# Collecting all output terms of a decode kernel in one PSUM bank, and multiplying the last matrix as it lands

## The chip, the cores and the metric

The kernel runs on one core of one Trainium2 chip. The metric is device time in microseconds (us), lower is better. Spans in a profile are a little shorter than the measured time (416.8 us of span beside 418.6 us). Each run of a changed kernel was taken on the same chip beside runs of the kernel before, and all runs quoted are marked fast in the record: none was more than 1.5% above the fastest of its kernel.

## The reference

One token passes through two branches whose results are added. Branch A is attention over a cache: 32 query heads share 4 key/value heads, with 65,536 cached positions of 128 numbers each. Branch B is a small MLP mixer. Everything is bf16.

```python
def _A_ref(x, k_cache, v_cache, wq, wo):           # x: 1 x 1 x 1024
    q = (x @ wq).reshape(1, 1, 32, 128)...
    p = softmax(q k^T * 128 ** -0.5)                 # 4 kv heads x 65536 positions
    return (p v).reshape(1, 1, 4096) @ wo            # wo: 4096 x 1024

def _B_ref(x, w1, w2, w3, w4):
    h = gelu(layernorm(x) @ w1)
    hs = shift(h) @ w2                               # one token: every shift moves in zeros
    x1 = x + hs
    return x1 + gelu(layernorm(x1) @ w3) @ w4        # w4: 3584 x 1024

xn = layernorm(x)
out = x + _A_ref(xn, ...) + _B_ref(xn, ...)
```

The caches are 134 MB, all matrices 36 MB. Each number is used once or a few times, so the transfers set the pace.

## The kernel before

Queues of operations are built per engine. `_deps` puts a wait into an engine's queue for every earlier writer and reader of a buffer. Note what it does not do: it does not leave out the engine's own semaphore. When a group of TensorE matmuls writes a buffer that the group before it, also on TensorE, wrote, TensorE waits for its own counter, that is until the earlier group is complete.

```python
def _deps(q, reads, writes):
    for b in reads:
        for s, v in b.w.items():
            q.wait((s, v))
    for b in writes:
        for s, v in b.w.items():
            q.wait((s, v))
        for s, v in b.r.items():
            q.wait((s, v))


def _done(ev, reads, writes, partial=False):
    for b in reads:
        b.add_read(ev)
    for b in writes:
        if partial:
            b.add_write(ev)
        else:
            b.set_write(ev)


def _op(q, fn, reads=(), writes=(), partial=False):
    _deps(q, reads, writes)
    ev = q.op(fn, True)
    _done(ev, reads, writes, partial)
    return ev


def _grp(q, fns, reads=(), writes=(), partial=False):
    _deps(q, reads, writes)
    ev = None
    for i, fn in enumerate(fns):
        ev = q.op(fn, i == len(fns) - 1)
    _done(ev, reads, writes, partial)
    return ev
```

The cache is handled in 32 blocks, eight for each kv head. After the last block of a head, `combine_1` and `combine_2` turn the running sums into that head's eight output columns `OTh_bf[:, h, :]`. They wait for `O_acc`, which GpSimd (POOL) finishes.

```python
def combine_1(h):
    _op(q_pe, lambda e: e.matmul(M0_ps[:, 0:1], Dmat_f[:, :], O_acc[:, 512:513], start=True, stop=True),
        reads=[b_Oacc, b_const], writes=[b_M0])
    _op(q_dve, lambda e: e.reciprocal(cb_rL[:, :], M0_ps[:, 0:1]), reads=[b_M0], writes=[b_cb])
    _op(q_dve, lambda e: e.tensor_scalar(out=cb_W4[:, :, :], in0=maskT[:, :, :], scalar1=cb_rL[:, 0:1], scalar2=None, op0=ALU.mult),
        reads=[b_cb, b_const], writes=[b_cb])

def combine_2(h):
    fns = []
    for t in range(4):
        fns.append(lambda e, t=t: e.matmul(M0_ps[:, 8:8 + G], O_acc[:, t * P:(t + 1) * P], cb_W4[:, t, :], start=(t == 0), stop=(t == 3)))
    _grp(q_pe, fns, reads=[b_Oacc, b_cb], writes=[b_M0])
    _op(q_dve, lambda e, h=h: e.tensor_copy(OTh_bf[:, h, :], M0_ps[:, 8:8 + G]), reads=[b_M0], writes=[b_OTh[h]])
```

The output projection takes one "wo row" at a time (128 x 1024 of `wo`): eight matmuls with the weights as stationary operand and one column as moving operand, all into one PSUM bank, one group for each row. I call these one-column matmuls.

```python
def wo_pe(h, g, src=None):
    if src is None:
        ws_ = (h * G + g) % NWO
        view, bufs = wo_sb[:, ws_, :], [b_wo[ws_]]
    else:
        view, bufs = src
    fns = []
    for ncx in range(KT_D):
        fns.append(lambda e, ncx=ncx, g=g, h=h, view=view: e.matmul(OA_ps[:, ncx:ncx + 1], view[:, ncx * P:(ncx + 1) * P], OTh_bf[:, h, g:g + 1],
                                                                  start=(g == 0 and ncx == 0), stop=(g == G - 1), skip_group_check=True))
    _grp(q_pe, fns, reads=bufs + [b_OTh[h]], writes=[b_OA], partial=(g > 0))
    if g == G - 1:
        _op(q_dve, lambda e: e.tensor_tensor(out=acc[:], in0=acc[:], in1=OA_ps[:, 0:KT_D], op=ALU.add), reads=[b_OA, b_acc], writes=[b_acc])
```

The w4 product has the same form. It comes in seven chunks of 512 x 1024, each one group of 32 matmuls.

```python
def mm_interleaved(ps_tile, col0, ncols, chunks, rhs_fn, b_rhs, b_ps, kt0=0, nkt_total=None):
    nkt = nkt_total if nkt_total is not None else sum(c[2] for c in chunks)
    first = (kt0 == 0)
    kt = kt0
    for sl, lhs_fn, kts in chunks:
        fns = []
        for kk in range(kts):
            for ncx in range(ncols):
                fns.append(lambda e, kk=kk, ncx=ncx, kt=kt, st=(first and kk == 0 and ncx == 0), lhs_fn=lhs_fn:
                           e.matmul(ps_tile[:, col0 + ncx:col0 + ncx + 1], lhs_fn(kk, ncx), rhs_fn(kt + kk),
                                    start=st, stop=(kt + kk == nkt - 1), skip_group_check=True))
        _grp(q_pe, fns, reads=sl.bufs + [b_rhs], writes=[b_ps], partial=not first)
        first = False
        kt += kts
```

At the end of the program, after the last head's combination, stand ten wo rows, then the seven w4 chunks, then an add, a transpose, a copy and the store:

```python
for (h_, g_) in wo_tail:
    wo_pe(h_, g_, src=wo_tail_src[(h_, g_)])
mm_interleaved(H2_ps, 0, KT_D, chunks_of("w4"), lambda kt: gh_bf[:, kt:kt + 1], b_gh, b_H2)
_op(q_dve, lambda e: e.tensor_tensor(out=fin[:], in0=acc[:], in1=H2_ps[:, 0:KT_D], op=ALU.add), reads=[b_acc, b_H2], writes=[b_fin])
_op(q_pe, lambda e: e.transpose(out=M0_ps[0:KT_D, 300:300 + P], in_=fin[:, :], identity=ident_f[:, :]), reads=[b_fin, b_const], writes=[b_M0])
_op(q_dve, lambda e: e.tensor_copy(orow[:, :], M0_ps[0:KT_D, 300:300 + P]), reads=[b_M0], writes=[b_orow])
```

```python
# ... cuts
ev_out = _dma(q_sp, ch_out, lambda e: e.dma_start(out=out[0, 0, :].rearrange("(kt p) -> kt p", p=P), in_=orow[:, :]), reads=[b_orow])
```

## Time and profile before

| | before |
|---|---|
| median of the first three runs | 418.62 us (418.47 to 418.73) |
| span of the profiled run | 416.8 us |
| moved from HBM | 169.9 MB, 408 GB/s over the span |
| last w4 chunk landed | about 406.7 us (issue at 385.2, landing 21.5 later) |
| last output matmul ended | about 414.2 us |

The slices of the page cut the span into 40 equal parts. A digit of 9 in the DMA row means that the transfer engines were at least 90% busy. PEclk is the clock granted to TensorE, in tenths.

```profile
span 416.8 us, 5862 instructions
...
PEclk9999955565565565555655555555555566556555
DMA  7999999999999999999999999999999999999980
GB/s 282 426 420 418 425 424 431 424 425 433 428 425 426 425 426 422 422 417 422 426 431 424 426 424 425 416 426 425 426 425 423 425 424 423 427 417 414 424 366 2
```

The transfers are full from the second slice to the 38th. Only the last two slices, about 21 us, are anything else: in the 39th the rate falls, in the 40th nearly nothing moves. What can be gained without moving fewer bytes lies there.

The timeline of the tail gives start (us), duration (us), engine, line, operation, output and inputs, and the idle time before with its releaser. PE stands for TensorE's matmuls, PEld for its weight loads, DVE for VectorE, POOL for GpSimd and SPq for the queue that issues transfers; "issue" means that the profile shows nothing that was waited for.

```profile
396.58 0.37 PE L558 MATMUL OA_ps<-OTh_bf,wo_sb 128*128 128x1 bf16 x8
...
398.52 0.59 PE L537 MATMUL M_ps<-O_acc,Dmat_f 128*128 128x1 f32 x2 [1.56 <-POOL O_acc L533]
...
399.64 1.88 PE L546 MATMUL M_ps<-cb_W,O_acc 128*128 128x8 f32 x8 [0.54 <-DVE cb_W L540]
...
402.58 0.35 PE L558 MATMUL OA_ps<-OTh_bf,WS 128*128 128x1 bf16 x8 [0.35 <-DVE acc L562]
...
406.08 0.35 PE L558 MATMUL OA_ps<-OTh_bf,WS 128*128 128x1 bf16 x8
...
406.29 0.99 PE L388 MATMUL H_ps<-gh_bf,WS 128*128 128x1 bf16 x32
...
413.13 0.99 PE L388 MATMUL H_ps<-gh_bf,Vn 128*128 128x1 bf16 x32
414.23 0.16 DVE L724 TENSOR_TENSOR fin<-acc,H_ps 128x8 f32<-128x8 f32 x1 [7.60 <-PE H_ps L388]
...
414.86 0.28 DVE L726 CAST orow<-M_ps 8x128 bf16<-8x128 f32 x1 [0.47 <-PE M_ps L725]
415.17 0.31 SPq L739 DMA_DIRECT2D out_dram<-orow  x1
```

The wo rows of the last head start after the combination, one every 0.50 us (0.35 of matmuls, the rest a gap). The first w4 chunk is multiplied at 406.29 us although it landed near 392.0. From there seven chunks take 1.14 us each, to 414.2 us.

The view of waits, for the weight loads of TensorE (PEld; total us, times, longest), shows the gaps of the wo rows without naming a cause:

```profile
PEld OA_ps L558 <- issue: 2.9, 10, 0.8
```

A stretch of the tail (us from and to, length, then busy us and number of instructions for PE, PEld, DVE, ACT and POOL, then the granted clock, DMA share and GB/s) shows the transfers running out while TensorE goes on at a clock of 0.50:

```profile
404.00:408.00 4.00, 3.17 (x94) 2.92 (x95) 0.16 (x1) 0.00 (x0) 0.00 (x0) 0.50 0.28 117
```

### The profile page before, as it was taken

To read this page: it belongs to the slowest core of one execution; us is meant where nothing else is said; L and a number is where in the kernel's file an instruction comes from. 1 tells how busy PE (TensorE), PEld (TensorE's weight loads), DVE (VectorE), ACT (ScalarE), POOL (GpSimd) and SP (SyncE) were. 2 spreads that over 40 slices of the span, in tenths; PEclk is the share of its full clock that TensorE was granted. 3 is DMA by queue.
4 is the path that set the end of the run, shared out by engine and by line. 5 is a ranking of instruction groups with operands and counts; after the bars stand their busy time and mean duration, and the time that the engine had idled before them with its cause. 6 is when DMAs were issued, how large, how long until landed. Compare 5 with 4: busy or idle time off the path is not lost.

```text
span 416.8 us, 5862 instructions
## 1 busy us (share of the span) xinstructions
PE 192.5 (46%) x2333; PEld 92.2 (22%) x2333; DVE 202.8 (49%) x369; ACT 84.7 (20%) x159; POOL 60.8 (15%) x86
## 2 busy tenths in 40 slices
PE   1532444434047646424464553345457543333566
PEld 1420111111015312101123221112224111111256
DVE  2037665625466476543345555344556655554200
ACT  0000322312122042221222221122222222121300
POOL 4000011111011121111110111111110111111210
PEclk9999955565565565555655555555555566556555
DMA  7999999999999999999999999999999999999980
GB/s 282 426 420 418 425 424 431 424 425 433 428 425 426 425 426 422 422 417 422 426 431 424 426 424 425 416 426 425 426 425 423 425 424 423 427 417 414 424 366 2
DMA packets 30330, 170.24 MB, mean 408 GB/s; under 512 B 2272, under 2 KB 2272, under 8 KB 23776
## 3 DMA queue, kind: packets, MB, share of 16 engines
q1 hardware_dynamic: 30304, 169.88, 97.8%
q8 instruction: 18, 0.29, 0.3%
q14 instruction: 8, 0.07, 0.0%
HBM read 169.87 MB, written 0.00 MB: 408 GB/s over the span
## 4 chain that ended last, share of the span: by engine, by line
DMA 43%; SPq 36%; PE 7%; DVE 6%; issue 4%; ACT 2%; POOL 0%; POOLq 0%; ACTq 0%; DVEq 0%
DMA Kn<-in_A_k_cache_dram 43%; SPq L435 22%; SPq L429 6%; SPq L422 4%; DVE X L448 3%; PE OT_ps L519 2%; ACT p_sb L490 2%; PE H_ps L388 2%; DVE mrow L467 1%; SPq L673 1%; SPq L342 1%; PE OA_ps L558 1%; PE M_ps L546 1%; PE PTB_ps L504 1%; SPq L579 1%
## 5 line engine op out<-in xcount | busy, mean ns | idle before, releaser
L448 DVE STREAM_TRANSPOSE X<-Kn 128x1024 f32<-128x1024 f32 x128 | 151.3, 1221 | 131.4 <-DMA Kn<-in_A_k_cache_dram 131.3
L490 ACT ACTIVATE p_sb<-S_ps,brun 128x512 bf16<-128x512 f32 x32 | 44.6, 1395 | 179.2 <-DVE brun L488 156.7
L519 PE MATMUL OT_ps<-Vn,pT_sb 128*32 128x512 bf16 x512 | 60.8, 627 | 22.0 <-ACT pT_sb L509 22.0
L460 PE MATMUL S_ps<-X,Yall 128*32 128x512 bf16 x512 | 59.1, 607 | 6.9 <-DVE X L448 6.9
L473 PE MATMUL PTB_ps<-Rm,Lmat 128*128 128x16 bf16 x32 | 6.2, 194 | 107.1 <-DVE Rm L468 107.1
L504 PE MATMUL PTB_ps<-ident_bf,p_sb 128*128 128x128 bf16 x128 | 19.2, 305 | 58.0 <-ACT ff L498 54.8
L533 POOL TENSOR_TENSOR O_acc<-O_acc,tmpO 128x513 f32<-128x513 f32 x28 | 32.8, 1172 | 88.5 <-ACT tmpO L527 88.5
L531 POOL TENSOR_SCALAR O_acc<-O_acc,ff 128x513 f32<-128x513 f32 x28 | 19.5, 698 | 169.1 <-ACT ff L498 169.1
L473 PEld LDWEIGHTS PTB_ps<-Rm,Lmat 128*128 128x128 bf16 x32 | 3.3, 104 | 131.7 <-DVE Rm L468 131.7
L527 ACT ACTIVATE tmpO<-OT_ps 128x512 f32<-128x512 f32 x32 | 19.1, 598 | 64.0 <-PE OT_ps L519 64.0
L519 PEld LDWEIGHTS OT_ps<-Vn,pT_sb 128*32 128x32 bf16 x512 | 14.9, 128 | 47.3 <-ACT pT_sb L509 30.4
L504 PEld LDWEIGHTS PTB_ps<-ident_bf,p_sb 128*128 128x128 bf16 x128 | 10.9, 129 | 60.6 <-ACT ff L498 57.3
L467 DVE TENSOR_REDUCE mrow<-S_ps 128x1 f32<-128x512 f32 x32 | 21.0, 657 | 5.7 <-PE S_ps L460 5.5
L509 ACT ACTIVATE pT_sb<-PTB_ps 128x512 bf16<-128x512 bf16 x32 | 19.1, 597 | 22.3 <-PE PTB_ps L504 22.3
L460 PEld LDWEIGHTS S_ps<-X,Yall 128*32 128x32 bf16 x512 | 15.9, 130 | 28.8 <-issue 21.5
L558 PEld LDWEIGHTS OA_ps<-OTh_bf,wo_sb 128*128 128x128 bf16 x176 | 6.4, 105 | 18.4 <-issue 18.4
L490 ACT ACT_TABLE_LOAD x1 | 1.3, 1283 | 43.3 <-DVE brun L485 43.3
L477 DVE TENSOR_REDUCE Bst<-PTB_ps 128x1 f32<-128x16 f32 x32 | 5.6, 175 | 8.4 <-PE PTB_ps L473 8.4
L529 POOL COPY O_acc<-tmpO 128x513 f32<-128x513 f32 x4 | 2.5, 614 | 48.4 <-ACT tmpO L527 48.4
L388 PE MATMUL H_ps<-xn_bf,WS 128*128 128x1 bf16 x224 | 8.6, 172 | 0.0
L490 ACT ACTIVATION_READ_ACCUMULATOR p_sb<-S_ps,brun 128x1 f32 x32 | 8.3, 259 | 0.0
L558 PE MATMUL OA_ps<-OTh_bf,wo_sb 128*128 128x1 bf16 x176 | 8.2, 168 | 0.0
(107 smaller groups left out, 123.2 us busy)
## 6 DMA issues: line engine op xcount, KB each, us to landing
Kn<-in_A_k_cache_dram SPq DMA_DIRECT2D x32, 2048.0 KB, 23.1
Vn<-in_A_v_cache_dram SPq DMA_DIRECT2D x32, 2048.0 KB, 26.3
WS<-in_B_w_dram SPq DMA_DIRECT2D x8, 896.0 KB, 19.2
wo_sb<-in_A_wo_dram SPq DMA_DIRECT2D x22, 256.0 KB, 25.2
WS<-in_B_w_dram SPq DMA_DIRECT2D x5, 1024.0 KB, 23.5
WS<-in_A_wq_dram SPq DMA_DIRECT2D x4, 1024.0 KB, 8.2
X<-in_A_wq_dram SPq DMA_DIRECT2D x4, 1024.0 KB, 17.0
Kn<-in_B_w_dram SPq DMA_DIRECT2D x4, 1024.0 KB, 15.9
```

What stands on the lines that cost most here:

```text
L429: _dma(q_sp, ch_v[s], lambda e, s=s, n=n: e.dma_start(out=Vn[:, s, :, :, :].rearrange("p a t d -> p a (t d)"), in_=kv_src(A_v_cache, n).re ...
L435: _dma(q_sp, ch_wo[ws_], lambda e, h=h, g=g, ws_=ws_: e.dma_start(out=wo_sb[:, ws_, :], in_=A_wo[(h * G + g) * DH:(h * G + g + 1) * DH, :] ...
L448: _op(q_dve, lambda e, ix=ix, ks=ks, xs=xs: e.transpose(out=X32[:, xs, 1024 * ix:1024 * (ix + 1)], in_=Kn32[:, ks, 16 * ix:16 * (ix + 1), ...
L460: fns.append(lambda e, we=we, c_mid=c_mid, mv=mv, h=h: e.matmul(S_ps[32 * c_mid:32 * c_mid + 32, :], Yall[:, h, we, :, :].rearrange("p a g ...
L467: _op(q_dve, lambda e, m=m: e.reduce_max(mrow[:, m:m + 1], S_ps[:, :], axis=AX.X), reads=[b_S], writes=[b_mrow[m]])
L490: _op(q_act, lambda e, n=n, m=m, kn=kn: e.activation(p_sb[:, m, :].rearrange("p (cl p0 ch) -> p cl ch p0", cl=4, p0=32), S_ps[:, :].rearra ...
L504: fns.append(lambda e, c2=c2, m=m: e.transpose(out=PT_ps[:, c2 * P:(c2 + 1) * P], in_=p_sb[:, m, c2 * P:(c2 + 1) * P], identity=ident_bf[:]))
L509: _op(q_act, lambda e, m=m: e.activation(pT_sb[:, m, :, :, :].rearrange("p r c g -> p c r g"), PT_ps[:, 0:512].rearrange("p (c r g) -> p c ...
L519: fns.append(lambda e, r=r, q4=q4, m=m, vs=vs: e.matmul(OT_ps[32 * q4:32 * q4 + 32, :], pT_sb[:, m, r, :, :].rearrange("p c g -> p (c g)") ...
L527: _op(q_act, lambda e, m=m: e.activation(tmpO[:, m, 0:512], OT_ps[:, :], ACTF.Copy), reads=[b_OT], writes=[b_tmpO[m]], partial=True)
L531: _op(q_pool, lambda e, m=m: e.tensor_scalar(out=O_acc[:, :], in0=O_acc[:, :], scalar1=ff[:, m, 0:1], scalar2=0.0, op0=ALU.mult, op1=ALU.add),
L533: _op(q_pool, lambda e, m=m: e.tensor_tensor(out=O_acc[:, :], in0=O_acc[:, :], in1=tmpO[:, m, :], op=ALU.add), reads=[b_tmpO[m]], writes=[ ...
```

## The change

The intent is to shorten that tail in three ways. All output terms (wo rows, w4 rows, residual) accumulate in one PSUM bank as rows, so that no separate add and transpose is needed: the activation column becomes the stationary operand, and the weights stream past it in four column strips of the array, 256 columns each, into partitions 0, 32, 64 and 96. W4 chunks 0 to 3 are multiplied before the last head's combination is complete. The output is copied from the bank and stored from its four rows.

```diff
@@ -345,6 +343,30 @@
             reads=[b_x8, b_const], writes=[b_M0])
         _op(q_dve, lambda e: e.tensor_copy(xT[:], M0_ps[:, 160:160 + KT_D]), reads=[b_M0], writes=[b_xT])
 
+        _op(q_dve, lambda e: e.memset(OUT_ps[:, :], 0.0), writes=[b_OUT])
+        out_started = [False]
+
+        def out_rows(items, reads, last=False):
+            fns = []
+            for lhs, view in items:
+                for jj in range(4):
+                    st = not out_started[0]
+                    fns.append(lambda e, lhs=lhs, view=view, jj=jj, st=st, last=last: e.matmul(
+                        OUT_ps[32 * jj:32 * jj + 1, 0:256], lhs, view[:, 256 * jj:256 * jj + 256],
+                        start=st, stop=last, tile_position=(0, 32 * jj), skip_group_check=True))
+                out_started[0] = True
+            _grp(q_pe, fns, reads=reads, writes=[b_OUT], partial=True)
+
+        def out_resid():
+            fns = []
+            for kt in range(KT_D):
+                jj, half = divmod(kt, 2)
+                fns.append(lambda e, kt=kt, jj=jj, half=half: e.matmul(
+                    OUT_ps[32 * jj:32 * jj + 1, half * P:(half + 1) * P], acc[:, kt:kt + 1], ident_f[:, :],
+                    start=False, stop=False, tile_position=(0, 32 * jj), skip_group_check=True))
+            assert out_started[0]
+            _grp(q_pe, fns, reads=[b_acc, b_const], writes=[b_OUT], partial=True)
+
         ln_uid = [0]
 
         def layer_norm(src, b_src, dst_f, dst_bf, b_dst, keep=None):
@@ -553,13 +575,7 @@
                 view, bufs = wo_sb[:, ws_, :], [b_wo[ws_]]
             else:
                 view, bufs = src
-            fns = []
-            for ncx in range(KT_D):
-                fns.append(lambda e, ncx=ncx, g=g, h=h, view=view: e.matmul(OA_ps[:, ncx:ncx + 1], view[:, ncx * P:(ncx + 1) * P], OTh_bf[:, h, g:g + 1],
-                                                                          start=(g == 0 and ncx == 0), stop=(g == G - 1), skip_group_check=True))
-            _grp(q_pe, fns, reads=bufs + [b_OTh[h]], writes=[b_OA], partial=(g > 0))
-            if g == G - 1:
-                _op(q_dve, lambda e: e.tensor_tensor(out=acc[:], in0=acc[:], in1=OA_ps[:, 0:KT_D], op=ALU.add), reads=[b_OA, b_acc], writes=[b_acc])
+            out_rows([(OTh_bf[:, h, g:g + 1], view)], bufs + [b_OTh[h]])
 
         def mk_loads(name, w, nkt, per):
             ncol = w.shape[1]
@@ -705,7 +721,7 @@
             PV(n)
             FLASH(n)
             run_pending(n, "c")
-            if nb == NB - 1:
+            if nb == NB - 1 and n + 1 < NBLK:
                 at(n + 1, "a", lambda h=h: combine_1(h))
                 at(n + 1, "b", lambda h=h: combine_2(h))
 
@@ -718,25 +734,28 @@
-        for (h_, g_) in wo_tail:
+        w4_ch = chunks_of("w4")
+
+        def w4_pe(i):
+            sl, _, kts = w4_ch[i]
+            kt = sum(c[2] for c in w4_ch[:i])
+            out_rows([(gh_bf[:, kt + kk:kt + kk + 1], sl.view[:, kk * D:(kk + 1) * D]) for kk in range(kts)],
+                     sl.bufs + [b_gh], last=(i == len(w4_ch) - 1))
+
+        for (h_, g_) in wo_tail[0:2]:
             wo_pe(h_, g_, src=wo_tail_src[(h_, g_)])
-        mm_interleaved(H2_ps, 0, KT_D, chunks_of("w4"), lambda kt: gh_bf[:, kt:kt + 1], b_gh, b_H2)
-        _op(q_dve, lambda e: e.tensor_tensor(out=fin[:], in0=acc[:], in1=H2_ps[:, 0:KT_D], op=ALU.add), reads=[b_acc, b_H2], writes=[b_fin])
-        _op(q_pe, lambda e: e.transpose(out=M0_ps[0:KT_D, 300:300 + P], in_=fin[:, :], identity=ident_f[:, :]), reads=[b_fin, b_const], writes=[b_M0])
-        _op(q_dve, lambda e: e.tensor_copy(orow[:, :], M0_ps[0:KT_D, 300:300 + P]), reads=[b_M0], writes=[b_orow])
... (the debugging taps, removed)
-        ev_out = _dma(q_sp, ch_out, lambda e: e.dma_start(out=out[0, 0, :].rearrange("(kt p) -> kt p", p=P), in_=orow[:, :]), reads=[b_orow])
+        out_resid()
+        for i in range(3):
+            w4_pe(i)
+        combine_1(HKV - 1)
+        w4_pe(3)
+        combine_2(HKV - 1)
+        for (h_, g_) in wo_tail[2:]:
+            wo_pe(h_, g_, src=wo_tail_src[(h_, g_)])
+        for i in range(4, len(w4_ch)):
+            w4_pe(i)
+        _op(q_dve, lambda e: e.tensor_copy(orow[:, :], OUT_ps[:, 0:256]), reads=[b_OUT], writes=[b_orow])
+        ev_out = _dma(q_sp, ch_out, lambda e: e.dma_start(out=out[0, 0, :].rearrange("(j n) -> j n", j=4), in_=orow[0:97:32, :]), reads=[b_orow])
```

Declarations (the bank `OUT_ps` in place of `OA_ps` and `H2_ps`, `orow` of 128 x 256) are left out.

More of the change, by code (lines that the diff above doesn't have):

```diff
@@ L234, in bass_parallel_sum__gqa_block_cached__mixer_s_mlp__decode_kernel @@
         gh_bf = sb("gh_bf", [P, KT_F], BF)
-        fin = sb("fin", [P, KT_D], F32)
-        orow = sb("orow", [KT_D, P], BF)
+        orow = sb("orow", [P, 256], BF)
         H3_ps = ps("H3_ps", [P, 512], F32)
-        H2_ps = H3_ps[:, 32:64]
-        OA_ps = ps("OA_ps", [P, 512], F32)
+        OUT_ps = ps("OUT_ps", [P, 512], F32)
         S_ps = ps("S_ps", [P, 512], F32)
@@ L265, in bass_parallel_sum__gqa_block_cached__mixer_s_mlp__decode_kernel @@
         b_X = [[_B() for _ in range(4)] for _ in range(2)]
-        b_H3 = _B(); b_H2 = _B(); b_tmpO = [_B(), _B()]
+        b_H3 = _B(); b_tmpO = [_B(), _B()]
         b_S = _B(); b_PT = _B(); b_MB = _B(); b_OT = _B()
@@ L275, in bass_parallel_sum__gqa_block_cached__mixer_s_mlp__decode_kernel @@
         b_wo = [_B() for _ in range(NWO)]
-        b_OA = _B()
+        b_OUT = _B()
         b_cb = _B()
@@ L608, in chunks_of @@
             return res
-        b_h1 = _B(); b_x1 = _B(); b_xn3 = _B(); b_gh = _B(); b_fin = _B(); b_orow = _B()
+        b_h1 = _B(); b_x1 = _B(); b_xn3 = _B(); b_gh = _B(); b_orow = _B()
         def mlp_early_1():
@@ L726, in bass_parallel_sum__gqa_block_cached__mixer_s_mlp__decode_kernel @@
-        _op(q_dve, lambda e: e.tensor_copy(orow[:, :], M0_ps[0:KT_D, 300:300 + P]), reads=[b_M0], writes=[b_orow])
-        if dbg:
-            taps = dict(xn=xn[:, :], qT_bf=qT_bf[:, :], Bst=Bst[:, :], Lst=Lst[:, :], O_acc=O_acc[:, :], maskT=maskT[:, :, :].rearrange("p t g -> p (t g)"),
-                        OTh_bf=OTh_bf[:, :, :].rearrange("p h g -> p (h g)"), acc=acc[:, :], fin=fin[:, :], p_sb=p_sb[:, :, :].rearrange("p m k -> p (m k)"),
-                        pT_sb=pT_sb[:, :, :, :, :].rearrange("p m r c g -> p (m r c g)"), hsT=x1[:, :], h1g=h1g_bf[:, :], gh=gh_bf[:, :],
-                        Yall=Yall[:, :, :, :, :].rearrange("p h w a g -> p (h w a g)"), X=X[:, 0, :], Lmat=Lmat[:, :], sel16=sel16[:, :], selG=selG_f[:, :])
-            ch_dbg = _DmaChan(sem("d_dbg"))
-            for qq in (q_pe, q_dve, q_act):
-                q_pool.wait((qq.sem, qq.cnt))
-            for name, dap in dbg.items():
-                src = taps[name]
-                _dma(q_pool, ch_dbg, lambda e, dap=dap, src=src: e.dma_start(out=dap, in_=src))
-                q_pool.wait((ch_dbg.sem, 16 * ch_dbg.n))
```

## The prediction

> **What bounds the kernel now.** The transfer queue, until the last twelve microseconds. The slices show DMA at 9 tenths and about 425 GB/s throughout; the stretches view gives DMA share 1.01 up to 402 us, 0.04 after 406. The rest of the 416.8 us span is a tail that TensorE bounds. By issue and landing, the seven w4 chunks land at about 392.0, 394.5, 396.9, 399.3, 401.8, 404.3 and 406.7 us. None is multiplied before 406.3: all stand behind the last head's wo rows, which stand behind that head's combination. The chain of waits: PV ends 396.65, O_acc ready 398.48, combination to 401.5, wo rows to 406.4 (0.36 + 0.14 us of gap each), seven w4 chunks to 414.2 (1.00 + 0.14 us each), add, transpose and copy to 415.14, store to 416.8.
>
> **What the change does.** The activation column becomes the stationary operand and the weights stream as rows: 4 matmuls of 256 columns in four column strips for 8 of one column. W4 chunks 0 to 3 fill the wait for the combination; the add and the transpose go.
>
> Cost of a row: the score matmuls, also in four strips, do 16 x 512 columns in 1.90 us at granted clock 0.50 (timeline), so strips run side by side (the Trainium skill, "TensorEngine Tiling (Array Packing)", Theoretical Speedup, says up to 4x; this agrees). So 4 x 256 columns should cost 1.90/8 = 0.24 us, an estimate: hardly less than the 0.28 us of a w4 row now, half the 0.50 us of a wo row. The gain is mostly order.
>
> New tail at clock 0.5 (estimates from those durations): the loop's wo row and two tail rows to 397.4; residual, 8 fp32 matmuls, about 2 us (least certain), to 399.4; w4 0-2 to 402.2; combine_1 0.6; w4 3 to 403.7; combine_2 1.9 to 405.6; cast 0.2; eight wo rows to 407.8; w4 4-6 to 410.5. Then the copy of 128x256 from PSUM, about 0.4 us (128x128 took 0.29), and the store's 1.66: span about 412.7, 4 us less.
>
> Clock: it rises to 1.0 at 343.6 and 377.7 us, each time after 3.4 us that PV and score matmuls filled over 93%; 77 to 80% did not raise it. The Trainium skill, "TensorE: Matmul & The Clock Gate", Part 1, gives such a window of about 3.4 us; the trace agrees. The old tail stayed at 0.5. The new one streams long rows, so the clock may rise near 401.6 us; if it holds, the matmuls end near 408, soon after the last landing. I give that even odds, in part or in full.
>
> Nothing else should move: transfers and what frees their buffers are unchanged, and the new memset (about 0.5 us) falls in a prologue waiting for wq.
>
> **Predicted: 413.4 us, 8 in 10 between 411.3 and 415.9.** Faster by over 2%: 0.03; within 2%: 0.96; slower by over 2%: 0.01. The last landing plus a last chunk, copy and store leaves about 411, so 2% is almost out of reach.
>
> **Right if** the last transfer still lands near 406.5; four w4 chunks precede combine_2; a w4 chunk takes 0.85-1.0 us (half if the clock rises); from the last matmul to the end is about 2.1 us, was 2.6.
>
> **Wrong if** the fp32 residual takes over 3.5 us; one-column stationary operands stop the strips from overlapping (a row would cost 0.9 us: slower by 15 us); switching between strips and full array drains the array; or the loop's shorter rows change the transfer stream.

## The result, and the profile after

| | before | after |
|---|---|---|
| median (same rounds) | 418.68 us (418.47 to 418.81, 4 runs) | 417.79 us (417.14 to 418.11, 4 runs) |
| ratio | | 0.998, 95% interval 0.9966 to 0.9994 |
| span of the profiled run | 416.8 us | 416.3 us |
| TensorE instructions (matmuls and loads) | 4666 | 4216 |
| last output matmul ended | 414.2 us | 413.7 us |
| from there to the end | 2.6 us | 2.6 us |

Ratios in this document are the mean time of one kernel's fast runs over that of the other's of the same rounds, so they are not quite the ratio of the medians.

The change is faster by 0.2%, where 1.3% was forecast. The slices after show the same stream of transfers:

```profile
span 416.3 us, 5407 instructions
...
PEclk9999996655655565666555555665555555665656
DMA  7999999999999999999999999999999999999990
GB/s 276 427 422 424 425 425 433 421 424 436 425 428 422 425 424 421 424 418 424 425 433 420 427 424 419 424 424 426 426 422 425 425 425 422 426 420 413 425 379 3
```

The tail after (columns as above):

```profile
396.67 0.38 PE L354 MATMUL OUT_ps<-WS,OTh_bf 128*1 128x256 bf16 x4 [0.16 <-PE OUT_ps L354]
...
397.68 1.06 PE L364 MATMUL OUT_ps<-ident_f,acc 128*1 128x128 f32 x16
...
398.94 1.02 PE L354 MATMUL OUT_ps<-WS,gh_bf 128*1 128x256 bf16 x16 [0.20 <-PE OUT_ps L364]
...
402.78 1.02 PE L354 MATMUL OUT_ps<-Kn,gh_bf 128*1 128x256 bf16 x16
...
403.73 1.88 PE L568 MATMUL M_ps<-cb_W,O_acc 128*128 128x8 f32 x8
...
405.91 0.38 PE L354 MATMUL OUT_ps<-WS,OTh_bf 128*1 128x256 bf16 x4 [0.30 <-issue]
...
406.46 0.38 PE L354 MATMUL OUT_ps<-WS,OTh_bf 128*1 128x256 bf16 x4 [0.17 <-PE OUT_ps L354]
...
410.29 1.02 PE L354 MATMUL OUT_ps<-Kn,gh_bf 128*1 128x256 bf16 x16 [0.17 <-PE OUT_ps L354]
...
412.66 1.02 PE L354 MATMUL OUT_ps<-Vn,gh_bf 128*1 128x256 bf16 x16 [0.17 <-PE OUT_ps L354]
413.74 0.42 DVE L757 CAST orow<-OUT_ps 128x256 bf16<-128x256 f32 x1 [7.92 <-PE OUT_ps L354]
414.19 0.62 SPq L758 DMA_DIRECT2D out_dram<-orow  x1
```

The order is as intended: w4 chunks 0 to 2 run from 398.94 us, chunk 3 between the two parts of the combination. But a wo row starts every 0.55 us, not every 0.24, and a w4 chunk every 1.18 us, not every 0.95. Both are a little longer than before the change. The waits, now with TensorE's matmuls (first) and weight loads (second):

```profile
PE OUT_ps L354 <- PE OUT_ps L354: 2.3, 14, 0.2
```

```profile
PEld OUT_ps L354 <- issue: 8.3, 16, 0.8
```

The first line says that matmuls into the bank waited for matmuls into the bank, 14 times. The second says that the loads of the next stationary columns, which but for the first row after the combination need only data long present, stood still 16 times for 8.3 us in all. The same stretch, to be held against that of before:

```profile
404.00:408.00 4.00, 3.13 (x24) 1.99 (x24) 0.17 (x1) 0.00 (x0) 0.00 (x0) 0.50 0.26 111
```

The clock was 0.50 here as before, and TensorE had work throughout. What the new order gains by filling the wait for the combination is lost again where the work itself got longer, and it had.

### The profile page after: what moved, and what is told of

Same layout as the page of the kernel before. It is cut to its first block, busy times and chain, and to the rows that moved or that the text cites. A ratio compares the mean times of both kernels' runs of the same rounds, so it can differ in the third digit from the quotient of the medians.

```text
span 416.3 us, 5407 instructions
## 1 busy us (share of the span) xinstructions
PE 191.5 (46%) x2108; PEld 87.1 (21%) x2108; DVE 202.4 (49%) x365; ACT 84.7 (20%) x159; POOL 60.7 (15%) x86
## 4 chain that ended last, share of the span: by engine, by line
SPq 45%; DMA 28%; PE 11%; DVE 8%; issue 4%; ACT 3%; POOL 0%; ACTq 0%; DVEq 0%; POOLq 0%
SPq L457 30%; DMA Kn<-in_A_k_cache_dram 24%; SPq L451 7%; DMA X<-in_A_wq_dram 5%; SPq L444 5%; DVE X L470 3%; PE OUT_ps L354 3%; PE OT_ps L541 3%; ACT p_sb L512 2%; DVE mrow L489 1%; SPq L595 1%; PE S_ps L482 1%; SPq L689 1%; PE PTB_ps L526 1%; PE M_ps L568 1%
## 5 line engine op out<-in xcount | busy, mean ns | idle before, releaser
L482 PEld LDWEIGHTS S_ps<-X,Yall 128*32 128x32 bf16 x512 | 18.4, 140 | 32.9 <-issue 24.9
L354 PE MATMUL OUT_ps<-wo_sb,OTh_bf 128*1 128x256 bf16 x88 | 9.5, 421 | 0.0
L410 PEld LDWEIGHTS H_ps<-xn_bf,WS 128*128 128x128 bf16 x224 | 8.1, 118 | 5.2 <-issue 5.2
```

What stands on the lines that cost most here:

```text
L354: fns.append(lambda e, lhs=lhs, view=view, jj=jj, st=st, last=last: e.matmul(OUT_ps[32 * jj:32 * jj + 1, 0:256], lhs, view[:, 256 * jj:256 ...
L482: fns.append(lambda e, we=we, c_mid=c_mid, mv=mv, h=h: e.matmul(S_ps[32 * c_mid:32 * c_mid + 32, :], Yall[:, h, we, :, :].rearrange("p a g ...
```

## The experiments

My first theory after the result (drain): each group of output matmuls waits for TensorE's own semaphore, because the group before it wrote the same bank. In that theory the wait empties the array and keeps the next loads from starting. Eight wo rows and three w4 chunks after the combination pay it eleven times. The rivals: one-column stationary operands and strips are slow by themselves (strips); or only the low clock is to blame (clock).

All runs, with medians in us:

| run | output matmuls | order | own waits | median | ratio to before |
|---|---|---|---|---|---|
| the change | rows | new | kept | 417.79 | 0.9980 |
| after_nodrain | rows | new | none | 413.20 | 0.9868 |
| before_nodrain | one-column | old | none | 416.23 | 0.9944 |
| order_only | one-column | new | kept | 416.03 | 0.9939 |
| rows_only | rows | old | kept | 418.83 | 1.0010 |
| after_split | rows | new | 21 more | 422.58 | 1.0098 |
| after_merged | rows | new | 7 fewer | 414.01 | 0.9884 |
| order_nodrain | one-column | new | none | 413.28 | 0.9875 |
| rows_old_order_nodrain | rows | old | none | 411.88 | 0.9844 |
| nodrain_pad | rows | new | none | 413.05 | 0.9874 |
| nodrain_lastsplit | rows | new | none | 412.50 | 0.9861 |
| nodrain_store8 | rows | new | none | 413.14 | 0.9875 |
| nodrain_fewer | rows | new | none | 411.53 | 0.9830 |
| nodrain_fewer_lastsplit | rows | new | none | 411.39 | 0.9827 |
| nodrain_store_wrong | rows | new | none | 412.57 | 0.9853 |

### after_nodrain: the own-semaphore waits taken out

The Trainium skill, "TensorE: Matmul & The Clock Gate", Part 2, says that matmuls stay in program order, so adding to the same bank should need no wait between TensorE's own groups. The wait for VectorE's memset stays, and so do all waits for data. The kernel is free of races by the simulator's check and gave a correct result, as did every other run without these waits except the store that is wrong on purpose; that agrees with the page.

```diff
+def _grp_nodrain(q, fns, reads=(), writes=()):      # as _grp, but for writes:
+    for b in writes:
+        for d in (b.w, b.r):
+            for s, v in d.items():
+                if s is not q.sem:
+                    q.wait((s, v))
 # in out_rows and out_resid:
-            _grp(q_pe, fns, reads=reads, writes=[b_OUT], partial=True)
+            _grp_nodrain(q_pe, fns, reads=reads, writes=[b_OUT])
```

> The changed kernel, except that a group of output matmuls no longer waits for TensorE's own semaphore, that is for the previous group into the same PSUM bank to have finished; all waits for data and for other engines stay. Theory (drain): a row costs 0.55 us instead of my 0.24 because each group waits until the one before has left the array, and a w4 chunk 1.18 instead of 0.95 for the same reason. Then eight wo rows after the combination take about 1.8 us instead of 4.4, a w4 chunk 0.87 instead of 1.18, the matmuls end near 408.3 instead of 413.7, and the time is about 412.4 us (411.3 if the denser stream also raises the clock). Rival (strips): one-column stationary operands or four strips writing one bank cost this by themselves, TensorE runs matmuls in order anyhow, and the wait is free: rows stay at 0.5 us and the time within 0.5 us of 417.8. Rival (clock): only the clock of 0.5 keeps it slow: nothing but a rise of the clock makes a row faster.

Measured: 413.2 us, 4.6 below the change. In its timeline the eight wo rows are one piece of 1.04 us, and TensorE then waits for w4 to land, twice:

```profile
401.62 1.04 PE L370 MATMUL OUT_ps<-WS,OTh_bf 128*1 128x256 bf16 x32 [0.35 <-DVE OTh_bf L586]
402.50 0.61 PE L370 MATMUL OUT_ps<-Kn,gh_bf 128*1 128x256 bf16 x16
404.19 0.61 PE L370 MATMUL OUT_ps<-Vn,gh_bf 128*1 128x256 bf16 x16 [1.08 <-DMA Vn<-in_B_w_dram]
407.93 1.02 PE L370 MATMUL OUT_ps<-Vn,gh_bf 128*1 128x256 bf16 x16 [3.14 <-DMA Vn<-in_B_w_dram]
```

In the waits of the weight loads, the 16 stops of 8.3 us have become one of 0.4 us:

```profile
PEld OUT_ps L370 <- issue: 0.4, 1, 0.4
```

The same part of that page says that TensorE pulls weight loads ahead of matmuls in flight, so that the next weights load while the matmul runs. These two lines agree with it, and show that a wait between the groups takes that away.

The clock rose too, from about 398.8 to 405.6 us, which it did not in the change's tail:

```profile
400.00:404.00 4.00, 2.75 (x64) 2.04 (x56) 0.33 (x2) 0.00 (x0) 0.00 (x0) 1.00 0.93 391
```

So the strips are not slow by themselves. Part of the shorter rows is the clock, though, so this run alone does not separate drain from clock. Two later runs do.

### after_split: 21 waits more

```diff
-            out_rows([(gh_bf[:, kt + kk:kt + kk + 1], sl.view[:, kk * D:(kk + 1) * D]) for kk in range(kts)],
-                     sl.bufs + [b_gh], last=...)
+            for kk in range(kts):
+                out_rows([(gh_bf[:, kt + kk:kt + kk + 1], sl.view[:, kk * D:(kk + 1) * D])],
+                         sl.bufs + [b_gh], last=...)
```

> A dose the other way: the changed kernel with every w4 chunk cut into four groups of 4 matmuls, each waiting for the group before it as the wo rows do. 21 more waits and nothing else, on a stretch where TensorE has no slack. Theory (drain): each costs the 0.33 us by which a wo row (0.55) exceeds a row inside a w4 group (0.21), so about 6.9 us more than the changed kernel, near 424.7 us. Rival (strips): the same matmuls, so still 417.8.

Measured: 422.58 us, 4.8 above the change, where 6.9 was expected. The clock was 0.50 in every microsecond of this tail from 395 to 412 us, so the clock has no part in it. Its timeline has a w4 chunk (first line) and a wo row (second):

```profile
398.47 1.74 PE L354 MATMUL OUT_ps<-WS,gh_bf 128*1 128x256 bf16 x16 [0.20 <-PE OUT_ps L364]
...
408.33 0.38 PE L354 MATMUL OUT_ps<-WS,OTh_bf 128*1 128x256 bf16 x4 [0.30 <-issue]
```

A chunk takes 1.90 us from start to start (1.74 and a gap of 0.16) instead of 1.18. Three waits more cost 0.72 us, that is 0.24 us each, and 21 of them 5.0. I had expected 0.33 because I took the whole excess of a wo row for it. A wo row waits for its own transfer as well; what the remaining 0.09 us is was not separated. Nor do the runs say what within the wait takes the 0.24 us, the array running empty or the semaphore's way back to TensorE: what they show is the cost of the wait.

### after_merged: seven waits fewer, none taken out of a group

```diff
-        for (h_, g_) in wo_tail[2:]:
-            wo_pe(h_, g_, src=wo_tail_src[(h_, g_)])
+        out_rows([(OTh_bf[:, h_, g_:g_ + 1], wo_tail_src[(h_, g_)][0]) for (h_, g_) in wo_tail[2:]],
+                 [b for hg in wo_tail[2:] for b in wo_tail_src[hg][1]] + [b_OTh[HKV - 1]])
```

> The changed kernel with every wait kept, but the last head's eight wo rows put into one group, so seven waits fewer. Theory (drain): the eight rows take about 2.0 us instead of 4.4, so near 415.5 us. Rival (strips): 417.8 still.

Measured: 414.01 us, but the four runs range from 411.45 to 415.15. In the profiled run (413.08 us) the eight rows are one piece of 1.69 us instead of 4.4, and the clock was up from 400.9 to 404.3 us and again from 407.7. The direction and the slow end of the range fit the theory. That the spread is the clock rising in some runs and not in others is likely but not shown, as only one run has a profile.

### order_only and rows_only: the two halves of the change

order_only is the kernel before with the new program order and nothing else. rows_only is the changed kernel with the old order.

```diff
 # order_only, against the kernel before:
-        for (h_, g_) in wo_tail: wo_pe(...)
-        mm_interleaved(H2_ps, 0, KT_D, chunks_of("w4"), ...)
+        for (h_, g_) in wo_tail[0:2]: wo_pe(...)
+        for i in range(3): w4_pe(i)
+        combine_1(HKV - 1)
+        w4_pe(3)
+        combine_2(HKV - 1)
+        for (h_, g_) in wo_tail[2:]: wo_pe(...)
+        for i in range(4, len(w4_ch)): w4_pe(i)
 # rows_only, against the changed kernel: these lines the other way, after the combination
```

> The kernel before with its one-column matmuls, its add and its transpose, but in the new program order: two tail rows, w4 chunks 0 to 2, combine_1, w4 3, combine_2, the other rows, w4 4 to 6. What the order alone is worth: with the durations of before, the matmuls end near 412.6 instead of 414.2, so about 417.1 us. If landings of w4 held the order back, it would stay at 418.7.

> The changed kernel's rows, residual, bank and store, in the old program order: combination first, then all wo rows, then all w4 chunks. Theory (drain): rows of 0.55 and chunks of 1.18 cost more than the old 0.50 and 1.14, plus the residual 1.26, so the matmuls end near 416.5 and the time is about 421 us, 2 us slower than before: the row form gives nothing and the order gives all. If the row form is worth something by itself, it is under 418.7.

Measured: order_only 416.03 us, 2.4 below before and 1.8 below the whole change. rows_only 418.83 us, the same as before within its interval (0.9993 to 1.0027). So with the waits in place the order gives the whole gain and the rows give some of it back. What the rows cost can be read from order_only's tail, beside the 4.38 us (eight rows, 405.91 to 410.29) of the change's:

```profile
404.22 3.85 PE L558 MATMUL OA_ps<-OTh_bf,WS 128*128 128x1 bf16 x64 [0.35 <-DVE OTh_bf L548]
```

Eight one-column rows take 3.85 us there, 3.71 from their start to that of the next chunk. The change also has the residual matmuls (1.26 us from start to next start) and a longer store (below), and saves the add and the transpose. rows_only came out 2 us better than I expected; its profile shows why, in the first w4 chunk and the last one:

```profile
407.33 1.02 PE L354 MATMUL OUT_ps<-WS,gh_bf 128*1 128x256 bf16 x16 [0.16 <-PE OUT_ps L354]
...
413.20 0.61 PE L354 MATMUL OUT_ps<-Vn,gh_bf 128*1 128x256 bf16 x16 [0.16 <-PE OUT_ps L354]
```

A chunk of 1.02 us becomes one of 0.61: the clock rose at 410.9 us in this run. In the change's profiled run it rose at 413.8, when the last matmul was done.

### before_nodrain and order_nodrain: one-column matmuls without the waits

The same waits taken out of wo rows and w4 chunks of the kernel before, in the old and in the new order.

```diff
-            _grp(q_pe, fns, reads=bufs + [b_OTh[h]], writes=[b_OA], partial=(g > 0))
+            (_grp_nodrain(q_pe, fns, reads=bufs + [b_OTh[h]], writes=[b_OA]) if g > 0 else _grp(...))
 # and likewise for the w4 chunks in mm_interleaved; order_nodrain adds the order of order_only
```

> The kernel before, with the same own-semaphore waits taken out of its wo rows and w4 chunks (rows of 8 one-column matmuls kept). Theory (drain): the old tail pays the same, a wo row 0.50 us instead of the 0.25 that 8 of a 32-matmul group take, a w4 chunk 1.14 instead of 1.0, so about 10 x 0.25 + 6 x 0.14 = 3.3 us less, 415.4 us. Rival (strips): the wait is free in both kernels, and the time stays within 0.5 us of 418.7.

> The kernel before with one-column matmuls, with the new order and without the own-semaphore waits: everything but the rows in one bank. If the row form gains by itself (fewer instructions, a faster clock), this stays slower than the 413.2 of the changed kernel without waits; if the gain is order and drains alone, it comes to about 413.5, since both then end on the last landing near 408. The clock should stay at 0.5 here, as in all one-column tails so far.

Measured: before_nodrain 416.23 us, so the kernel before paid for the waits as well. Eight of its one-column wo rows take 1.71 us (401.89 to 403.60) at clock 0.50, 0.214 us each where they were 0.50. It stayed 0.8 above the expected 415.4: its timeline has a gap of 1.7 us inside a w4 chunk, at 406.1 us, in which TensorE waited for nothing that the profile shows, and one of 0.45 us at 411.4 us.

```profile
401.89 1.85 PE L574 MATMUL OA_ps<-OTh_bf,WS 128*128 128x1 bf16 x64 [0.35 <-DVE acc L578]
403.60 0.99 PE L404 MATMUL H_ps<-gh_bf,WS 128*128 128x1 bf16 x32
...
407.82 2.03 PE L404 MATMUL H_ps<-gh_bf,Kn 128*128 128x1 bf16 x71 [1.71 <-issue]
...
411.83 0.33 PE L404 MATMUL H_ps<-gh_bf,Vn 128*128 128x1 bf16 x7 [0.45 <-issue]
```

Between the ends of the two gaps lie 128 matmuls and 128 weight loads, 256 instructions, and each gap ended 1.4 us after a 16 KB packet on the instruction queue had ended (at 406.4 and 410.4 us; these packets are the subject of a later section). So TensorE was probably out of instructions. No run tests that.

order_nodrain 413.28 us, the same as after_nodrain's 413.20. Without the waits and in the new order, the form of the matmuls makes no difference to the time. The clock did differ, as one line for the whole tail of order_nodrain shows: TensorE busy 9.73 of 11.5 us and the clock 0.50.

```profile
396.50:408.00 11.50, 9.73 (x286) 9.57 (x283) 0.90 (x5) 0.32 (x1) 1.09 (x1) 0.50 0.74 309
```

One-column matmuls at 85% did not raise it (nor did the 3 us from 397 to 400 us, which they, their loads and combine_1 filled), and streams of 256 columns did. Both kernels end alike because both wait for the last w4 chunk at the end. Where that wait is not the end, the form does matter: see the next run.

### rows_old_order_nodrain: is the order still worth something?

The old order of rows_only, without the waits.

> The changed rows without own-semaphore waits, in the old program order (all output matmuls after the combination). From 401.3 us: ten rows 2.2, residual 0.9, 28 w4 rows 6.0 at clock 0.5, less if the clock rises in that dense stretch: matmuls end at 408.5 to 410.4, time 413.3 to 414.8. Then the order, worth 1.0 to 2.4 us with the waits in place, is worth under 1 us without them, since the last landing near 408 is the floor. If order is worth the same always, it is about 415.5.

Measured: 411.88 us, 1.3 below after_nodrain, which has the new order. This separates drain from clock. The first line is the eight wo rows, the second w4 chunk 0; the clock was 0.50 up to 405.0 us.

```profile
402.31 1.92 PE L370 MATMUL OUT_ps<-WS,OTh_bf 128*1 128x256 bf16 x32
404.02 1.07 PE L370 MATMUL OUT_ps<-WS,gh_bf 128*1 128x256 bf16 x16
```

From 402.31 to 404.02 us eight rows take 1.71 us, 0.214 us each at clock 0.50, against 0.55 with the waits at the same clock. So a row in a stream costs what the strips allow (I had said 0.24), and the clock is not needed for it. It also matters which end comes last. TensorE was through at about 407.7 us in the old order, and after_nodrain could not be, because its last chunk was not there before 407.9 us. That is a transfer question, and the next runs ask it.

Beside before_nodrain (416.23 us), which differs from this run in the form of the output terms alone (rows, bank, residual, store), the rows are worth 4.4 us. From the start of the first w4 chunk to the end of the last it is 3.7 us here (404.02 to 407.7) and 8.6 there (403.60 to 412.2). Of these 4.9 us, 2.2 are the two gaps; most of the rest came with the clock, which rose here at 405.0 us and stayed at 0.50 there.

### nodrain_pad, nodrain_lastsplit: the last landing

In the transfer records of each trace I looked at the 16 completions of the last w4 chunk. In the change 15 and 16 are 0.2 us apart; in after_nodrain the last comes 1.3 us after the fifteenth (406.55 and 407.89 us). The records also show packets of 16 KB on an instruction queue, 0.9 us long, 18 in the kernel before (4666 TensorE instructions), 17 in the change (4216). That is one for about 256 TensorE instructions, and agrees with the Trainium skill, "Runtime: NRT & Kernel Launch", Instruction fetch mechanics, which says that an engine's instruction memory is refilled in blocks of 16 KiB, 256 instructions, through a transfer queue, and that this is "mostly hidden". In after_nodrain one of them falls into the end of the stream. The list of queues for 402 to 406.5 us of after_nodrain (packets, MB, share of the 16 engines):

```profile
q1 hardware_dynamic: 162, 1.13, 60.2%
q8 instruction: 1, 0.02, 1.3%
```

nodrain_pad adds 108 one-column matmuls to the prologue to move that fetch; nodrain_lastsplit loads the last chunk in four.

```diff
 # nodrain_pad
+        _grp(q_pe, [lambda e: e.matmul(M1_ps[:, 511:512], ident_bf[:, :], ident_bf[:, 0:1], start=True, stop=True)
+                    for _ in range(108)], reads=[b_const], writes=[b_M1])
 # nodrain_lastsplit
-            _dma(q_sp, sl.chan, ... out=sl.view[:, 0:per * ncol], in_=ld["src"] ...)
+            for kk in range(4):                       # last chunk only, one semaphore and one buffer record each
+                _dma(q_sp, ch_w4l[kk], ... out=sl.view[:, kk * D:(kk + 1) * D],
+                     in_=B_w4[(KT_F - 4) * P:KT_F * P, :].rearrange("(p kk) n -> p kk n", kk=4)[:, kk, :] ...)
```

> The changed kernel without own-semaphore waits, plus 108 matmuls of one column into an unused place early in the prologue, where TensorE waits for wq. In the runs without waits TensorE waited for the last w4 chunk until 407.9 us, and where that happened a 16 KB packet of TensorE's own instructions had been fetched at about 405, while the last w4 bytes were on their way; in the changed kernel with waits it was fetched at 400.5 and the last landing came 1.1 us earlier. The 216 instructions more shift the moment of that fetch and change nothing in the tail. Theory (fetch): the last chunk starts near 406.8 and the time falls from 413.2 to about 412.2 us. Rival: the late landing is chance or due to the order, and the time stays within 0.4 us of 413.2.

> The changed kernel without own-semaphore waits, the last w4 chunk loaded as four transfers of 256 KB in place of one of 1 MB, each row multiplied as it lands. If the tail is now bound by the last landing, three of the four rows (0.6 us of 1.05) are out of the way before it: about 412.5 us against 413.2. If TensorE is still the bound, no change.

Measured: nodrain_pad 413.05 us, no gain: the last chunk still started at 407.75 us. As I put it, the theory failed. The 17th fetch had moved to 399.7 us, and the last completion was still 1.3 us late. nodrain_lastsplit 412.50 us, as expected: the last row alone, 0.28 us, was left after the last landing. The tail without waits is bound by the landing.

What did go with the late completion in all runs by then was not when a fetch came but how many had come before the end of the stream. In the seven kernels with 17 or more, the last completion was 1.2 to 1.4 us late. In the six with 16, counting the kernel before and rows_old_order_nodrain, whose 17th came as the last data landed, it was within 0.24 us. (The text on record below says five, and 1.1 to 1.3 us; the traces give the figures here.) The change has 16 by then and after_nodrain 17, only because TensorE is through its program sooner. nodrain_pad had made matters no better, since 216 more instructions mean one fetch more.

### nodrain_fewer, nodrain_fewer_lastsplit: one fetch less

With one token every shift in branch B moves in zeros, so the 64 w2 matmuls multiply zeros. Leaving 48 out changes no result; w2 is still loaded. (This is an instrument here, not a proposal.)

```diff
-            mm_interleaved(M1_ps, 72, KT_D, chunks_of("w2"), ...)
+            mm_interleaved(M1_ps, 72, KT_D, [(sl, f, 1) for (sl, f, k) in chunks_of("w2")], ...)
```

> The changed kernel without own-semaphore waits, and with 48 of the 64 w2 matmuls left out at period 8 (they multiply a vector of zeros, as the sequence has one token, so the result stays correct; w2 is still loaded). 96 TensorE instructions fewer and nothing else. In the trace records of the runs so far, seven kernels that had 17 or more 16 KB instruction fetches before the transfers ended got the last of the 16 completions of the last w4 chunk 1.1 to 1.3 us after the fifteenth; five that had 16, or whose 17th came after the data, within 0.2 us. 108 more matmuls (one fetch more) did not help. Theory (one fetch too many): with 96 fewer the 17th falls after the end, the last chunk starts near 406.8 instead of 407.9, and the time is 412.0 us. Rival: a late transfer engine by chance; 413.1 us.

> The same, with the last w4 chunk in four transfers. Theory (one fetch too many): the last row lands near 406.7 and takes 0.3 us, matmuls end near 407.0, time about 411.3 us, below all so far. Rival: 412.5 as without the shortened prologue.

Measured: nodrain_fewer 411.53 us, 1.7 below after_nodrain. There were 16 fetches in all, and the 16th completion came 0.03 us after the fifteenth. In the same stretch of its trace the instruction queue is missing, where after_nodrain had one packet, and its last chunk starts at 406.43 us instead of 407.93:

```profile
q1 hardware_dynamic: 167, 1.16, 61.3%
```

```profile
406.43 0.90 PE L370 MATMUL OUT_ps<-Vn,gh_bf 128*1 128x256 bf16 x16 [1.80 <-DMA Vn<-in_B_w_dram]
```

The count of fetches forecast this run, which a late completion by chance would not have done. nodrain_store_wrong (below), with 17 again, had it 1.4 us late again.

Why does the 17th hurt and the 16th not? I had looked at the last chunk only; the completions of the earlier transfers, which every trace keeps, answer it in the main. In each of the 16 traces, transfers that landed between the first fetch and the second had their last completion 1.0 to 1.5 us behind the fifteenth, and so had those between the ninth and the tenth, by 0.9 to 1.4 us. After every other fetch up to the 16th the distance was at most 0.52 us. So the 17th is the third of a series with a step of eight: the first fetch of each eight makes one completion later than all others, and the seven that follow make others as late (in after_nodrain one after the first fetch, two after the second). This fits fetches that go round eight of the 16 transfer engines in turn. The records do not say which engine moved a packet, so the engines are an inference; the step of eight is not.

nodrain_fewer_lastsplit 411.39 us is the fastest of all, 1.7% below the kernel before, but only 0.1 below nodrain_fewer. Its last row started at 406.75 us: with four small transfers the last bytes came 0.3 us later than with one, which ate half of the gain.

### nodrain_store8 and nodrain_store_wrong: the store

```diff
-  out=out[0, 0, :].rearrange("(j n) -> j n", j=4), in_=orow[0:97:32, :]
+  out=...rearrange("(j h n) -> j h n", j=4, h=2), in_=orow[0:97:32, :].rearrange("j (h n) -> j h n", h=2)   # store8
+  out=...rearrange("(j n) -> j n", j=4), in_=orow[0:4, :]                                                # store_wrong
```

> The changed kernel without own-semaphore waits, its output stored in 8 pieces of 256 B in place of 4 of 512 B, from the same four partitions. From the end of the last copy to the end of the span it is 2.1 us in the changed kernel, 1.66 before, and the issue of the store takes 0.62 us against 0.31. If the number of pieces does it, the issue falls to 0.31 and the time by about 0.4 us to 412.8; if it is the partition step of 32 rows, it stays at 0.62 and 413.2.

> Wrong on purpose: the changed kernel without own-semaphore waits, its store reading partitions 0 to 3 in place of 0, 32, 64 and 96. If the partition step makes the store's issue 0.62 us instead of 0.31, it falls to about 0.31 and the time by 0.3 to 0.4 us from 413.1; if not, both stay, and the longer store stays unexplained.

Measured: with 8 pieces the issue still took 0.61 us, and the time was 413.14 us, unchanged. With four neighbouring partitions (the result is wrong, on purpose) the issue took 0.29 us:

```profile
409.35 0.29 SPq L774 DMA_DIRECT2D out_dram<-orow  x1
```

The time was 412.57 us, 0.6 below after_nodrain (another set of rounds, where the kernel before had a median of 418.50 against 418.45). In the profiled runs 0.48 us of this lie between the end of the copy and the end of the span (2.10 us in after_nodrain, 1.62 here), 0.33 of them in the issue. So it is the step of 32 partitions that makes the store's issue 0.3 us longer, not the number of pieces.

## Why the prediction was wrong, point by point

The tail in terms of the prediction, from the chain of waits of the change (start to next start):

| term | predicted, us | measured, us |
|---|---|---|
| three wo rows before the residual | 0.75 | 1.38 |
| residual | 2.0 | 1.26 |
| w4 0 to 2 | 2.8 | 3.39 |
| combine_1, w4 3, combine_2 | 3.4 | 3.28 |
| cast, until the first row | 0.2 | 0.30 |
| eight wo rows | 2.0 | 4.38 |
| w4 4 to 6 | 2.7 | 3.42 |
| copy | 0.4 | 0.42 |
| store | 1.66 | 2.1 |

- **What bounds it: right.** Transfers to 402 us, then TensorE. The stream of transfers did not change.
- **"4 x 256 columns should cost 1.90/8 = 0.24 us": this step failed.** It is right for a row in a stream (0.214 us at clock 0.50, rows_old_order_nodrain), and wrong for a row that is a group of its own. I took the rate from 16 matmuls inside one group and applied it to groups of four, each of which waits for the one before to be complete. The old tail showed the same thing, "0.36 + 0.14 us of gap each", and I wrote the gap down and then left it out of the sum for the new tail. The profiled span missed the forecast 412.7 by 3.6 us. Eight wo rows are 2.4 of it, six w4 chunks outside the combination 1.3, the first three rows 0.6, the store 0.4; the residual gave 0.7 back, and the tail had begun 0.35 us earlier than forecast. Of the "right if" list, a w4 chunk of 0.85 to 1.0 us failed for the same reason: one started every 1.18 us.
- **"Hardly less than the 0.28 us of a w4 row now, half the 0.50 us of a wo row": the second half was wrong** for the same reason. A row costs no less than before while the waits are there, and without them both forms take 0.214 us at clock 0.50 and end alike in the new order (413.28 against 413.20 us). In the old order without waits rows end 4.4 us earlier (411.88 against 416.23), mostly by the clock and the two gaps of before_nodrain.
- **"The gain is mostly order": right, and more than right.** Order alone gave 2.4 us, more than the whole change.
- **Clock, "even odds, in part or in full": it did not rise** until 413.8 us. Without the waits it rose in time in every profiled version with rows. But the waits do not exclude a rise: with most of them in place it rose in rows_only (410.9 us) and in after_merged (400.9 and 407.7). In all traces the clock changes at moments a whole number of 3.41 us apart. In the change the stretch with most of the wo rows (406.9 to 410.3 us) was filled to 69% and no rise followed; the next, with three w4 chunks and their waits, was filled to 88%, and the rise came too late to help. Filling does not decide alone: the stretch from 400.1 to 403.5 us was filled to 95%, with combine_1 in it, and no rise followed. Where these stretches fall differs from run to run, so part of this was luck.
- **Landing, near 406.5: right for the change.** As a floor for faster versions it was 1.4 us too early (407.9 in after_nodrain), because of one more instruction fetch. That the change itself had only 16 by then, and landed on time, was luck.
- **From the last matmul to the end, "about 2.1 us": it was 2.6.** The copy was right; the store was 0.4 us longer, of which 0.3 is the issue from partitions 32 apart.
- **None of my "wrong if" items came true.** The residual took 1.26 us, strips overlapped, full-array and strip matmuls alternated at the combination without a visible cost, and the transfer stream was the same.

What remains open: whether the gaps in before_nodrain are missing instructions, the spread of after_merged, and which engines the fetches go through.

## What to carry to other kernels

When you cost a new group of operations with a rate read from an old one, carry over its waits too: a helper that orders every write after every earlier write makes an engine wait for itself, and here the change gained 0.9 us with those waits and 5.3 us without them. Look in the waits for an engine that waits for its own output, and for weight loads that stand still on "issue"; in-order accumulation on one engine needs no such wait, or the pieces can be put into one group. Once the compute tail is short, ask what the next floor is (here a late last transfer), and give it its own experiment before believing in it.

## What the Trainium skill lacked or had wrong

- "TensorE: Matmul & The Clock Gate", Part 2, says that loads are pulled ahead of matmuls in flight, and that a single isolated matmul costs more than one in a stream, but not that a wait on TensorE's own semaphore between two groups into one bank isolates every group so, nor what that costs: 0.24 us for each group of four 256-column matmuls at clock 0.50 (after_split), and 0.55 against 0.214 us for a wo row with its other wait.
- The same page, Part 1, speaks of a busy window without saying what counts as busy: here one-column matmuls, busy 9.73 of 11.5 us, left the clock at 0.50, and 256-column streams raised it to 1.0. In the kernel before, two stretches of 3.4 us that PV and score matmuls filled to 93 and 96% raised it, but two filled to 96% with one-column matmuls among them (125.2 to 128.6 and 135.4 to 138.8 us) did not.
- "Runtime: NRT & Kernel Launch", Instruction fetch mechanics, calls the refill of instructions "mostly hidden". On a kernel that fills the transfer engines it was not always: a 17th packet (0.9 us) before the end of the stream went with a last completion 1.2 to 1.4 us late, and the last chunk started at 407.93 instead of 406.43 us. The first and the ninth packet had made one completion of every transfer late in the same way.
- "DMA: Bandwidth & Descriptors" does not say that a store from partitions 32 apart takes longer to issue: 0.62 us from partitions 0, 32, 64, 96, 0.29 us from 0 to 3, 0.31 us from eight neighbours.
